# The last ten units of an attention kernel with a gated MLP: how the softmax sums, the PV lag and the last four output tiles are scheduled

## The chip, the cores and the metric

The kernel runs on one core of one Trainium2 chip. The metric is the device time in microseconds (us); the median of 3 runs is 1253.81 us (1253.02 to 1254.78).

## The reference

Everything is bf16 at the interface, with a sequence of 2048 tokens, a width of 512, 32 heads of 128 and 2048 cached keys.

```python
xn = layernorm(x)                                   # 2048 x 512
q = (xn @ wq) -> 32 heads x 2048 x 128
p = softmax(q @ k_cache.T * 128**-0.5)              # per head 2048 x 2048
s = concat_heads(p @ v_cache) @ wo                  # 2048 x 512
h = gelu(layernorm(xn) @ w1)                        # four column groups shifted by 1, -1, 2, -2 tokens
x1 = xn + shifted(h) @ w2
B = x1 + gelu(layernorm(x1) @ w3) @ w4              # width 1792 in between
out = x + s * silu(B)
```

## The kernel before

**Units and slots.** Attention is cut into 128 units of one head and 512 queries: `units` runs over 8 groups of four heads, in each over four query blocks (`qt`), in each over the four heads (`hh`). A unit has 8 slots (`SPU`), so the main loop has `NS` = 1024 of them. Below, 126.4 is slot 4 of unit 126. In each slot `s_slot` issues two score matmuls (128 keys by 512 queries each) into a two-bank PSUM tile from `psS` (two such tiles), and ScalarE turns them into `pT` with one exponential of 128x1024. `pv_slot` issues the two matmuls P times V of a slot that lies `LAG` or more slots back; `LAGS` lists the lag by position: 5 at the beginning, 10 in the long middle part, and back from 10 to 5 over units 120 to 122. Beside them a slot may carry matmuls of the next Q projection (`q_mm`, slots 0 and 1), of the output projection of one 128-token tile (`wo_mm`, slots 4 and 5), and pieces of the MLP (`chunks`, which run out in unit 119).

**Order.** All instructions are pinned to program order on their engine; the order is written out by the loop over `n`. What is put with `at(n, ...)` is issued at the end of slot n.

**Softmax sums.** VectorE adds the four `pT` tiles of a unit (`add_first`, `add_next` 2 and 3) and folds the result to 128x512 (`fold`). The sum over the 128 key partitions is then taken in one of two ways:

- *Turned units* (`turned(u)`: 4 <= u < `T1`, `T1` = 118): the folded tile is transposed by a DMA (`acc_turn`), VectorE reduces it to 128x4 (`turned_sums`) and takes the reciprocal, `dr` goes to DRAM, and `bcast` brings it back to all partitions (`rb`, 256 KB). `norm` of such a unit comes at slot 7 of unit u+2.
- *Other units* (0 to 3 and 118 to 127): `sums` issues four matmuls of one column each with `ones_t` and takes the reciprocal; `dr` and `rb` go by DMA in the same way, and `norm` comes at slot 2 of unit u+2.

The last unit has no folded tile: `split_sums` issues 40 one-column matmuls on the unfolded tiles between the last PV matmuls, and `bcast` follows.

**Output.** When the fourth head of a query block is normalised (`normed`), its four token tiles join `wo_todo`; `wo_mm` accumulates four heads in one PSUM bank and `wo_post` adds the bank to `s_acc`. For group 6, query blocks 2 and 3 are `deferred`: their `oT` goes to DRAM (`o_d`), comes back in `tail_open` as `oS`, and is accumulated into the same bank as group 7, which makes eight matmuls for tiles 8 to 15. In group 7 a tile is finished by `wo_out` (gate, residual, DMA out; `fin_load` brings its gate and residual). For tiles 12 to 15 `gate_sum` prepares `s_acc`, and the code behind the loop ends them with `last_scale` and `last_out`: tiles 12, 13 and 14 with 512 columns (the last add of 12 and 13 on GpSimd), tile 15 in two halves of 256. `tail_open` issues ten loads on SP at 121.0.

Of the kernel before, what the change touches and what calls it, by code (L numbers as in the profile page):

```python
# [17 lines left out]
def kernel(  # L18
# [102 lines left out]
    def mm(out, lhsT, rhs, start, stop):  # L121
        mm_count[0] += out.shape[-1] / 512
        pin(nc.tensor.matmul(out=out, lhsT=lhsT, rhs=rhs, start=start, stop=stop))  # L123
# [13 lines left out]
    LAGS = [(T0 * SPU + 4 * (i + 1), LAG + i) for i in range(5)] + [((T1 + 2) * SPU + 2, LAG + 5)]  # L137
    LAGS += [((T1 + 2) * SPU + 6 + 4 * i, LAG + 4 - i) for i in range(4)] + [(NS, LAG)]
# [95 lines left out]

    def sums(u):
        s = st[u]
        ps = psX.tile([P, 4], FP32, tag="xm" if u + 1 == QUIET - 1 else "xa", name="ps_sum")
        a = s["acc"][:, 0, :].rearrange("k (p j) -> k j p", j=4)
        for j in range(4):
            mm(ps[:, j:j + 1], a[:, j, :], ones_t[:], True, True)  # L240
        recip(s, ps)

    def recip(s, ps):
        rc = smp.tile([P, 4], FP32, name="rc")
        pin(nc.vector.reciprocal(out=rc[:], in_=ps[:]))
        s["dr"] = drp.tile([P, 4], FP32, name="dr")
        pin(nc.sync.dma_start(out=s["dr"][:], in_=rc[:]))

    def turned(u):
        return T0 <= u < T1  # L250
# [10 lines left out]
            out=sm[:], in_=s.pop("at")[:], axis=mybir.AxisListType.X, op=ALU.add))  # L261
        recip(s, sm)

    def split_sums(u, parts):
        s = st[u]
        if "ps" not in s:
            s["ps"] = psX.tile([P, 4], FP32, tag="xm", name="ps_sum")
        for a, first, last in parts:
            a = a.rearrange("k (p j) -> k j p", j=4)
            for j in range(4):  # L270
                mm(s["ps"][:, j:j + 1], a[:, j, :], ones_t[:], first and j == 0, last and j == 3)
        if parts[-1][2]:
            recip(s, s["ps"])

    def bcast(u):
        st[u]["rb"] = rp.tile([P, 512], FP32, name="rb")
# [20 lines left out]
    wo_box = {}  # L297

    def wo_mm(g, t, hhs, tag="xa"):
        if hhs[0] == 0:  # L300
            wo_box[0] = psX.tile([P, D], FP32, tag=tag, name="ps_wo")
        held = g == NG - 1 and (NG - 2, t // 4) in deferred
        if held and hhs[0] == 0:
            wo_part(wo_box[0][:], g - 1, t, range(HG), True, False)
        wo_part(wo_box[0][:], g, t, hhs, hhs[0] == 0 and not held, hhs[-1] == HG - 1)
# [10 lines left out]
    def tail_open():  # L316
        ph.close()
        ph3 = ph.enter_context(pool("ph3", reuse_waits="tile"))
        for g, qt in deferred:
            oTs[(g, qt)] = ph3.tile([P, HG, 512], BF16, name=f"oS{qt}")  # L320
            pin(nc.sync.dma_start(out=oTs[(g, qt)][:], in_=o_d[qt][:]))
        for t in range(4 * LQ, NT):
            gf = ph3.tile([P, D], BF16, name=f"gf{t}")
            pin(nc.sync.dma_start(out=gf[:], in_=g_d[t][:]))
            xf = ph3.tile([P, D], BF16, name=f"xf{t}")
            pin(nc.sync.dma_start(out=xf[:], in_=xsrc[t]))
            tl[t] = (gf, xf)

    def gate_sum(t):
        gf, xf = tl[t]  # L330
        sa = s_acc[:, t, :]
        pin(nc.vector.scalar_tensor_tensor(
            out=sa, in0=sa, scalar=0.5, in1=gf[:], op0=ALU.mult, op1=ALU.mult))
        pin(nc.vector.tensor_tensor(out=sa, in0=sa, in1=xf[:], op=ALU.add))

    def last_scale(t, ps, cs=slice(0, D)):
        gf, xf = tl[t]
        pin(nc.vector.scalar_tensor_tensor(  # L338
            out=gf[:, cs], in0=ps, scalar=0.5, in1=gf[:, cs], op0=ALU.mult, op1=ALU.mult))
# [15 lines left out]
    def wo_post(g, t):  # L355
        ps = wo_box.pop(0)
        sa = s_acc[:, t, :]
        if g == 0:
            pin(nc.vector.tensor_copy(out=sa, in_=ps[:]))
            return  # L360
        pin(nc.vector.tensor_tensor(out=sa, in0=ps[:], in1=sa, op=ALU.add))  # L361
# [409 lines left out]
            at((b - 4 - hh // 2) * SPU + (5, 7)[hh % 2], lambda h=h: load_wo(h))  # L771

    at(QUIET * SPU, tail_open)
    for t in range(4 * LQ, NT):
        if t % 4 < 2:
            at((QUIET + 1 + 2 * (t % 4)) * SPU + 4, lambda t=t: gate_sum(t))

    wo_todo = deque()
    pv_done = 0
# [11 lines left out]
    for n in range(NS):  # L791
# [33 lines left out]
            acc_turn(u - 1)  # L825
        if p == 2 and u >= 2 and turned(u - 2):
            bcast(u - 2)
        if p == (4 if u == T1 + 2 else 2) and u >= 2 and not turned(u - 2):
            normed(u - 2)
        if p == 3 and u >= 1 and not turned(u - 1):  # L830
            sums(u - 1)
        if p == 4 and u >= 1 and u != T1 + 1 and not turned(u - 1):
            bcast(u - 1)
        if p in (4, 5) and wo_todo:
            wo_mm(*wo_todo[0], (0, 1) if p == 4 else (2, 3))
# [9 lines left out]
        if u == QUIET - 1 and p >= 6:  # L845
            wo_mm(*wo_todo[0], (0, 1) if p == 6 else (2, 3), "xm")
            if p == 7:
                gg, t = wo_todo.popleft()
                wo_post(gg, t)
                at(n + 5, lambda t=t: wo_out(t))  # L850
        if p == 4:
            add_first(u)
        if p == 4 and u == NU - 1:
            a = st[u]["acc"]
            pin(nc.vector.tensor_tensor(out=a[:, 0:2, :], in0=a[:, 0:2, :], in1=a[:, 2:4, :], op=ALU.add))
        if p == 6 and u < QUIET:
# [26 lines left out]
            debt[0] += SMALL  # L883
        if p == SPU - 1 and u >= 2 and turned(u - 2):
            normed(u - 2)
        if p == SPU - 1 and u == T1 + 1:
            bcast(T1)
    while act_late:
        act_late.popleft()(NS)
    late = [fn for n in sorted(todo) for fn in todo[n]]  # L890
    assert min(todo) >= NS and not chunks and len(wo_todo) == 1
    U = NU - 1
    GL = NG - 1
    s = st[U]
    gg, t11 = wo_todo.popleft()
    ts = [4 * LQ + j for j in range(4)]
    norm(U - 1)
    held = range(HG)
    ready = range(HG - 1)
    pv_slot(U, 3)  # L900
    split_sums(U, [(s["acc"][:, i, :], i == 0, False) for i in range(2)]
               + [(s["pT"][2][:, i, :], False, False) for i in range(4)])
    pv_slot(U, 4)
    split_sums(U, [(s["pT"][3][:, i, :], False, False) for i in range(2)])
    pv_slot(U, 5)
    split_sums(U, [(s["pT"][3][:, i, :], False, i == 3) for i in range(2, 4)])
    bcast(U)
    for fn in late:
        fn()
    for t in ts[2:]:  # L910
        gate_sum(t)
    pv_slot(U, 6)
    pv_slot(U, 7)
    wo_mm(gg, t11, (0, 1, 2, 3))
    wo_post(gg, t11)
    wo_out(t11)
    pa = psS.tile([P, 2, 512], FP32, name="ps_s")
    pb = psS.tile([P, 2, 512], FP32, name="ps_s")
    pc = psX.tile([P, D], FP32, tag="xa", name="ps_wo")
    dst = [pa[:, 0, :], pb[:, 0, :], pc[:]]  # L920
    halves = [psX.tile([P, D], FP32, tag="xm", name="ps_wo"), psO.tile([P, D], FP32, tag="ps_o", name="ps_wo")]
    for j in (0, 1):
        wo_part(dst[j], GL - 1, ts[j], held, True, False)
        wo_part(dst[j], GL, ts[j], ready, False, False)
    wo_part(dst[2], GL - 1, ts[2], held, True, False)
    norm(U, 2)
    for j in (0, 1):
        wo_part(dst[j], GL, ts[j], (HG - 1,), False, True)
        last_scale(ts[j], dst[j])
        last_out(ts[j], nc.gpsimd)  # L930
    wo_part(dst[2], GL, ts[2], range(HG), False, True)
    last_scale(ts[2], dst[2])
    last_out(ts[2], nc.vector)
    for i, queue in enumerate((nc.sync, nc.scalar)):
        cs = slice(i * D // 2, (i + 1) * D // 2)
        ps = halves[i][:, cs]
        wo_part(ps, GL - 1, ts[3], held, True, False, cs)
        wo_part(ps, GL, ts[3], range(HG), False, True, cs)
        last_scale(ts[3], ps, cs)
        last_out(ts[3], nc.vector, cs, queue)  # L940
    ph.close()


# [28 lines left out]
```

## Time and profile before

| | us |
|---|---|
| median of 3 runs | 1253.81 |
| the profiled execution: its time | 1253.69 |
| the profiled execution: its span | 1251.9 |
| PE busy | 1242.8 (99%) |
| DVE busy (VectorE) | 1107.5 (88%) |
| ACT busy (ScalarE) | 1130.6 (90%) |
| POOL busy (GpSimd) | 139.5 (11%) |

The span goes from the first to the last instruction; 1.8 us of the time lie around it. L123 is the line of the matmul helper, so matmuls are told apart by their tiles. Busy times of one engine overlap a little: an instruction starts before the one in front of it has drained, so what a queue takes is read from start to start in the timeline (a 128x512 addition on VectorE lasts 0.69 us and the next one starts 0.60 us after it).

### The profile page before, as it was taken

Reading aid. Unit: us, or ns where it says so; the run is one execution under the profiler, and the core shown is the slowest. Engines: PE = TensorE matmul, PEld = TensorE weight load, DVE = VectorE, ACT = ScalarE, POOL = GpSimd, SP = SyncE. Lnnn points to the kernel's source line nnn. Section 1 sums busy time; section 2 is a strip of 40 time slices with the busy share of each in tenths; the row PEclk is TensorE's granted clock in tenths of the full one; section 3 lists DMA queues with packets and bytes.
Section 4 is the critical chain, followed back from the end, with each engine's and each line's share of the span. In section 5 each row is a group of like instructions: output and inputs, shape, how many; then the busy total and the mean of one; then the engine's idle time right before and its main releaser. Section 6 shows DMA issues by size and latency. Waiting matters only on the chain.

```text
span 1251.9 us, 16586 instructions
## 1 busy us (share of the span) xinstructions
PE 1242.8 (99%) x5872; PEld 599.1 (48%) x5872; DVE 1107.5 (88%) x1509; ACT 1130.6 (90%) x1285; POOL 139.5 (11%) x239
## 2 busy tenths in 40 slices
PE   9999999999999999999999999999999999999998
PEld 5444444444444444444444444444444444444444
DVE  7899999999899988899988889999888999888887
ACT  7999998888999888899988889998888999988893
POOL 4410003332101000000100000010000000000111
PEclk9999999999999999999999999999999999999999
DMA  9654444565635555344663345554535343564532
GB/s 185 136 114 88 78 106 80 118 149 109 135 72 114 118 95 102 61 91 90 111 126 76 69 93 97 110 71 108 97 89 108 66 89 81 115 134 74 154 72 69
DMA packets 235108, 126.70 MB, mean 101 GB/s; under 512 B 186832, under 2 KB 212048, under 8 KB 235024
## 3 DMA queue, kind: packets, MB, share of 16 engines
q1 hardware_dynamic: 225920, 100.40, 41.8%
q0 software_dynamic: 8672, 24.91, 7.9%
q8 instruction: 46, 0.75, 0.3%
q14 instruction: 38, 0.31, 0.1%
q10 hardware_dynamic: 432, 0.33, 0.1%
HBM read 82.58 MB, written 7.60 MB: 72 GB/s over the span
## 4 chain that ended last, share of the span: by engine, by line
PE 96%; DMA 1%; ACT 1%; DVE 1%; issue 0%; SPq 0%; POOL 0%; POOLq 0%; DVEq 0%
PE ps_s L123 35%; PE ps_o L123 34%; PE ps_m L123 10%; PE ps_q L123 9%; PE ps_wo L123 8%; ACT pT L207 1%; DMA dr<-rc 1%; DMA w_sb<-in_B_w_dram 0%; DMA rb<-dr 0%; PE ps_sum L123 0%; DVE gf L338 0%; DVE xf L343 0%; ACT pre L528 0%; DVE qT L193 0%; DVE bn L384 0%
## 5 line engine op out<-in xcount | busy, mean ns | idle before, releaser
L207 ACT ACTIVATE pT<-ps_s 128x1024 bf16<-128x1024 f32 x1024 | 1024.4, 1028 | 99.2 <-PE ps_s L123 88.7
L123 PE MATMUL ps_s<-qT,kT 128*128 128x512 bf16 x2048 | 608.9, 379 | 0.9 <-ACT pT L207 0.5
L123 PE MATMUL ps_o<-pT,vb 128*128 128x512 bf16 x2048 | 608.0, 379 | 0.3 <-DVE oT L294 0.3
L123 PEld LDWEIGHTS <-kT 128*128 128x128 bf16 x2048 | 231.1, 113 | 226.1 <-issue 4.9
L218 DVE TENSOR_TENSOR acc<-acc,pT 128x2048 bf16<-128x2048 bf16 x254 | 306.4, 1206 | 10.1 <-ACT pT L207 9.9
L123 PEld LDWEIGHTS <-vb 128*128 128x128 bf16 x2048 | 200.0, 98 | 225.8 <-DMA vb<-in_A_v_cache_dram 0.5
L213 DVE TENSOR_TENSOR acc<-pT 128x2048 bf16<-128x2048 bf16 x128 | 156.2, 1220 | 31.8 <-ACT pT L207 31.6
L123 PE MATMUL ps_q<-xnT,wq_h 128*128 128x512 bf16 (+1 forms) x524 | 152.8, 374 | 0.8 <-ACT xnT L459 0.6
L123 PE MATMUL ps_wo<-wo_h,oT 128*128 128x512 bf16 (+1 forms) x476 | 140.2, 377 | 0.2 <-DVE qT L193 0.2
L287 DVE TENSOR_TENSOR oT<-ps_o,rb 128x512 bf16<-128x512 f32 x114 | 122.3, 1073 | 8.9 <-DMA rb<-dr 8.9
L361 DVE TENSOR_TENSOR s_acc<-ps_wo,s_acc 128x512 f32<-128x512 f32 x100 | 68.7, 687 | 43.5 <-PE ps_wo L123 43.2
L222 DVE TENSOR_TENSOR acc<-acc 128x1024 bf16<-128x1024 bf16 x127 | 86.8, 683 | 0.9
L193 DVE CAST qT<-ps_q 128x512 bf16<-128x512 f32 x109 | 74.9, 688 | 8.7 <-PE ps_q L123 7.7
L123 PEld LDWEIGHTS <-wq_h 128*128 128x128 bf16 x524 | 50.8, 98 | 61.1 <-issue 1.3
L260 DVE TENSOR_REDUCE sm<-accT 128x4 f32<-128x512 bf16 x114 | 77.5, 680 | 0.5 <-DMA accT<-acc 0.2
L123 PE MATMUL ps_m<-xn2T,w_sb 128*128 128x512 bf16 x224 | 77.1, 379 | 0.0
L123 PE MATMUL ps_m<-w_sb,h2T 128*128 128x512 bf16 x224 | 77.1, 379 | 0.0
L123 PEld LDWEIGHTS <-oT 128*128 128x128 bf16 x484 | 47.3, 98 | 57.6 <-DVE oT L294 1.4
L659 POOL DMA_DIRECT2D w_sb<-in_B_w_dram x28 | 21.1, 754 | 370.4 <-PE ps_m L123 370.4
L687 POOL DMA_DIRECT2D g_d<-xr x16 | 8.7, 546 | 442.3 <-DVE xr L685 376.5
L223 DVE TENSOR_TENSOR acc<-acc 128x512 bf16<-128x512 bf16 x127 | 54.0, 425 | 4.4
L496 DVE SCALAR_TENSOR_TENSOR sq<-sq,pre 128x1024 bf16<-128x1024 bf16 x36 | 44.0, 1221 | 3.9 <-ACT sq L492 3.9
(89 smaller groups left out, 602.9 us busy)
## 6 DMA issues: line engine op xcount, KB each, us to landing
rb<-dr SPq DMA_DIRECT2D x128, 256.0 KB, 4.2
vb<-in_A_v_cache_dram SPq DMA_DIRECT2D x64, 256.0 KB, 3.6
w_sb<-in_B_w_dram POOLq DMA_DIRECT2D x28, 256.0 KB, 3.8
wo_h<-in_A_wo_dram SPq DMA_DIRECT2D x32, 128.0 KB, 3.0
wq_h<-in_A_wq_dram SPq DMA_DIRECT2D x28, 128.0 KB, 3.1
kT<-in_A_k_cache_dram SPq DMA_TRANSPOSE x128, 3.4
dr<-rc SPq DMA_DIRECT2D x128, 2.0 KB, 1.6
xr<-in_A_x_dram POOLq DMA_DIRECT2D x16, 128.0 KB, 2.5
```

The source lines that it names most:

```text
L123: pin(nc.tensor.matmul(out=out, lhsT=lhsT, rhs=rhs, start=start, stop=stop))
L193: pin(nc.vector.tensor_copy(out=qT[:], in_=st[u].pop("psq")[:]))
L207: pin(nc.scalar.activation(out=s["pT"][-1][:, jj:jj + 2, :], in_=sps[:], func=ACT.Exp, scale=SCALE))
L213: pin(nc.vector.tensor_tensor(out=s["acc"][:], in0=s["pT"][0][:], in1=s["pT"][1][:], op=ALU.add))
L218: pin(nc.vector.tensor_tensor(out=a[:], in0=a[:], in1=st[u]["pT"][i][:], op=ALU.add))
L222: pin(nc.vector.tensor_tensor(out=a[:, 0:2, :], in0=a[:, 0:2, :], in1=a[:, 2:4, :], op=ALU.add))
L223: pin(nc.vector.tensor_tensor(out=a[:, 0, :], in0=a[:, 0, :], in1=a[:, 1, :], op=ALU.add))
L260: pin(nc.vector.tensor_reduce(out=sm[:], in_=s.pop("at")[:], axis=mybir.AxisListType.X, op=ALU.add))
L287: pin(nc.vector.tensor_tensor(out=oTs[(g, qt)][:, hh, :].rearrange(f, j=4), in0=s["o"].rearrange(f, j=4), in1=s["rb"].rearrange("x (p j) - ...
L361: pin(nc.vector.tensor_tensor(out=sa, in0=ps[:], in1=sa, op=ALU.add))
L496: pin(nc.vector.scalar_tensor_tensor(out=sq[:].rearrange(f2), in0=sq[:].rearrange(f2), scalar=1.0, in1=pre[:].rearrange(f2), op0=ALU.add, ...
L659: pin(nc.gpsimd.dma_start(out=w[:], in_=w3_v[:, :, fc * P:(fc + 2) * P]))
```

## The change

- `T1` becomes 126: units 118 to 125 are turned units too. Only 126 still uses `sums`, at slot 4 of unit 127, with `bcast` at slot 5.
- The lag stays at 10 to the end of the loop, so ten PV slots (126.6, 126.7 and all of 127) come after it, where there were five.
- Unit 127 is summed by six matmuls of 512 columns with a 128x128 tile of ones (`ones_p`): the result stands in all partitions at once. VectorE takes the reciprocal of 128x512 from PSUM into `rb`; no DMA is in this path.
- Tiles 12 to 15 are all done in halves of 256 columns, each half in a PSUM bank of its own, each with `last_scale` and `last_out` on VectorE and its DMA out on SP or ACT in turn. GpSimd does no addition there. All of it stands behind the last PV matmul; before, most matmuls of tiles 12 to 14 stood ahead of the last `norm`.
- Unit 120 no longer carries two output tiles; tiles 0 to 3 go to units 118 to 121, 4 to 7 to 122 to 125, 8 and 9 to 126 and 127, 10 and 11 behind the loop. In 126 and 127 the held half of a tile goes to slots 2 and 3.
- The tail's loads are issued one pair at a time, at slot 5 of units 121 to 126; `gate_sum` of tiles 14 and 15 moves from behind the loop to 126.4 and 127.2. The last unit's third addition is made (`add_next(u, 2)` at 127.6).

```diff
-    T0, T1 = 4, NU - 10
...
+    T0, T1 = 4, NU - 2
+    LAGS = [(T0 * SPU + 4 * (i + 1), LAG + i) for i in range(5)] + [(NS, LAG + 5)]
...
-    def split_sums(u, parts):
+    def split_sums(u, parts, first, last):
         s = st[u]
...
+        if first:
+            s["ps"] = psS.tile([P, 2, 512], FP32, name="ps_s")[:, 0, :]
+        for i, a in enumerate(parts):
+            mm(s["ps"], tl["ones"][:], a, first and i == 0, last and i == len(parts) - 1)
+        if last:
+            s["rb"] = tl["rb"].tile([P, 512], FP32, tag="rb3", bufs=2, name="rb")
+            pin(nc.vector.reciprocal(out=s["rb"][:], in_=s["ps"]))
...
+    loads = [lambda t=t: gate_load(t) for t in range(4 * LQ, NT)]
+    for i, (g, qt) in enumerate(deferred):
+        loads.insert(2 + 3 * i, lambda g=g, qt=qt: held_load(g, qt))
+    for i, load in enumerate(loads):
+        at((QUIET + i) * SPU + 5, load)
     for t in range(4 * LQ, NT):
...
+        at((QUIET + 1 + 2 * (t % 4)) * SPU + 4 if t < NT - 1 else NS - 6, lambda t=t: gate_sum(t))
...
+        if p == (4 if u > T1 else 3) and u >= 1 and not turned(u - 1):
             sums(u - 1)
...
+        if p in (2, 3) and u >= NU - 2:
+            wo_held(*wo_todo[0], (0, 1) if p == 2 else (2, 3))
...
+        if p == 6 and u == NU - 1:
+            add_next(u, 2)
             a = st[u]["acc"]
             pin(nc.vector.tensor_tensor(out=a[:, 0:2, :], in0=a[:, 0:2, :], in1=a[:, 2:4, :], op=ALU.add))
...
+    acc = [s["acc"][:, i, :] for i in range(2)]
+    pT3 = [s["pT"][3][:, j, :] for j in range(4)]
+    split_sums(U, pT3[:2], True, False)
+    pv_slot(U - 1, 6)
+    split_sums(U, pT3[2:], False, False)
+    pv_slot(U - 1, 7)
+    late_sums = lambda: split_sums(U, acc, False, True)
     for fn in late:
         fn()
...
+    for tag in ("xa", "xm"):
+        gg, t = wo_todo.popleft()
+        wo_mm(gg, t, range(HG), tag)
+        if wo_todo:
+            late_sums()
+        wo_post(gg, t)
+        wo_out(t)
+        if wo_todo:
+            fin_load(t + 1)
+            norm(U - 1)
+    for p in range(SPU):
+        pv_slot(U, p)
     norm(U, 2)
...
+    parts = [(t, c, c + D // 2, q) for t in ts for c, q in ((0, nc.sync), (D // 2, nc.scalar))]
+    for (t, c0, c1, queue), ps in zip(parts, banks):
+        cs = slice(c0, c1)
+        wo_part(ps[:, cs], GL - 1, t, range(HG), True, False, cs)
+        wo_part(ps[:, cs], GL, t, range(HG), False, True, cs)
+        last_scale(t, ps[:, cs], cs)
+        last_out(t, nc.vector, cs, queue)
```

More of the change, by code (lines that the diff above doesn't have):

```diff
@@ L236, in sums @@
         s = st[u]
-        ps = psX.tile([P, 4], FP32, tag="xm" if u + 1 == QUIET - 1 else "xa", name="ps_sum")
+        ps = psX.tile([P, 4], FP32, tag="xa", name="ps_sum")
         a = s["acc"][:, 0, :].rearrange("k (p j) -> k j p", j=4)
@@ L262, in turned_sums @@
         recip(s, sm)
-    def split_sums(u, parts):
+    def split_sums(u, parts, first, last):
         s = st[u]
[L266 to L273, printed above, removed]
+        if first:
[5 more added lines that the diff above has]
+            pin(nc.vector.reciprocal(out=s["rb"][:], in_=s["ps"]))
     def bcast(u):
-        st[u]["rb"] = rp.tile([P, 512], FP32, name="rb")
+        st[u]["rb"] = (tl["rb"].tile([P, 512], FP32, tag="rb3", bufs=2, name="rb") if u >= T1 else rp.tile([P, 512], FP32, name="rb"))
         pin(nc.sync.dma_start(
@@ L299, in wo_mm, with wo_held @@
     def wo_mm(g, t, hhs, tag="xa"):
+        held = g == NG - 1 and (NG - 2, t // 4) in deferred
+        if held and 0 not in wo_box:
+            wo_held(g, t, range(HG), tag)
+        if hhs[0] == 0 and not held:
+            wo_box[0] = psX.tile([P, D], FP32, tag=tag, name="ps_wo")
+        wo_part(wo_box[0][:], g, t, hhs, hhs[0] == 0 and not held, hhs[-1] == HG - 1)
+    def wo_held(g, t, hhs, tag="xm"):
         if hhs[0] == 0:
             wo_box[0] = psX.tile([P, D], FP32, tag=tag, name="ps_wo")
[L302 to L305, printed above, removed]
+        wo_part(wo_box[0][:], g - 1, t, hhs, hhs[0] == 0, False)
     def wo_part(ps, g, t, hhs, first, last, cs=slice(0, D)):
@@ L318, in tail_open, with held_load, gate_load @@
         ph3 = ph.enter_context(pool("ph3", reuse_waits="tile"))
+        tl["rb"] = ph3
+        tl["ones"] = ph3.tile([P, P], BF16, name="ones_p")
+        pin(nc.gpsimd.memset(tl["ones"][:], 1.0))
         for g, qt in deferred:
             oTs[(g, qt)] = ph3.tile([P, HG, 512], BF16, name=f"oS{qt}")
-            pin(nc.sync.dma_start(out=oTs[(g, qt)][:], in_=o_d[qt][:]))
         for t in range(4 * LQ, NT):
[L323 to L327, printed above, removed]
+            tl[t] = [ph3.tile([P, D], BF16, name=f"{name}{t}") for name in ("gf", "xf")]
+    def held_load(g, qt):
+        pin(nc.sync.dma_start(out=oTs[(g, qt)][:], in_=o_d[qt][:]))
+    def gate_load(t):
+        for tile_, src in zip(tl[t], (g_d[t][:], xsrc[t])):
+            pin(nc.sync.dma_start(out=tile_[:], in_=src))
     def gate_sum(t):
@@ L890 @@
     late = [fn for n in sorted(todo) for fn in todo[n]]
-    assert min(todo) >= NS and not chunks and len(wo_todo) == 1
+    assert min(todo) >= NS and not chunks and len(wo_todo) == 2
     U = NU - 1
@@ L894 @@
     s = st[U]
-    gg, t11 = wo_todo.popleft()
     ts = [4 * LQ + j for j in range(4)]
[L897 to L906, printed above, removed]
@@ L918 @@
[L918 to L925, printed above, removed]
-    norm(U, 2)
[L927 to L930, printed above, removed]
@@ new lines @@
+    for p in range(SPU):
+        pv_slot(U, p)
+    norm(U, 2)
+    sb = [psS.tile([P, 2, 512], FP32, name="ps_s") for _ in range(2)]
+    banks = [b[:, 0, :] for b in sb]
+    banks += [psX.tile([P, D], FP32, tag=tag, name="ps_wo")[:] for tag in ("xa", "xm")]
+    banks += [psO.tile([P, D], FP32, tag="ps_o", name="ps_wo")[:] for _ in range(2)]
+    banks += [b[:, 1, :] for b in sb]
+    parts = [(t, c, c + D // 2, q) for t in ts for c, q in ((0, nc.sync), (D // 2, nc.scalar))]
[5 more added lines that the diff above has]
+        last_out(t, nc.vector, cs, queue)
```

39 lines of the change are left out of this document (3 added, 36 removed).

## The prediction

> **What bounds the kernel now.** I read the page first, then the chain of waits of the last 27 us, then the timeline of the last ten units, engine by engine.
>
> ```profile
> PE 1242.8 (99%) x5872; PEld 599.1 (48%) x5872; DVE 1107.5 (88%) x1509; ACT 1130.6 (90%) x1285; POOL 139.5 (11%) x239
> ...
> 1236.77 0.19 DVE rc L245
> 1236.98 2.64 DMA dr<-rc
> 1239.69 3.43 DMA rb<-dr
> 1243.14 0.44 DVE oT L294
> 1243.63 0.40 PE ps_s L123
> 1244.05 1.90 DVE gf L338 x3
> 1245.97 1.68 DVE xf L343
> 1247.65 0.35 DVE gf L338
> 1248.02 0.42 DVE xf L343
> ```
>
> TensorE is the bound almost everywhere: a 512-column matmul starts every 0.2157 us, and from 1139.8 to 1236 all gaps together are about 0.6 us. So only three things can move the time: matmul work, the gaps, and what stands behind the last matmul. The chain shows the one large gap: the last unit's sums go out and back by DMA (6.2 us), `norm` starts at 1243.14, and PE, which ran out of other work at 1243.06, goes on at 1243.63 (0.57 us lost). The end is VectorE's alone:
>
> ```profile
> 1244.83 2.27 POOL L343 TENSOR_TENSOR xf<-gf,s_acc 128x512 bf16<-128x512 bf16 x2 [19.08 <-DVE gf L338]
> 1245.97 1.68 DVE L343 TENSOR_TENSOR xf<-gf,s_acc 128x512 bf16<-128x512 bf16 x1
> 1246.24 0.60 PE L123 MATMUL ps_wo<-wo_h,oT 128*128 128x256 bf16 x4
> 1249.27 0.35 ACTq L344 DMA_DIRECT2D out_dram<-xf  x1
> ```
>
> The last four half matmuls (0.110 us each) end at 1246.68, the last DMA is issued at 1249.27: 2.59 us. VectorE's addition of 128x512 took 1.68 us while GpSimd did the same kind of addition; the same shape in L368 took 0.425.
>
> **The change, part by part; gains.**
> 1. Sums of 118 to 125 leave PE. From the timeline of unit 127:
>
> ```profile
> 1228.67 0.27 PE L123 MATMUL ps_sum<-ones_t,acc 128*128 128x1 bf16 x4
> 1228.80 0.60 PE L123 MATMUL ps_s<-qT,kT 128*128 128x512 bf16 x2
> ```
>
> They take 0.13 us of PE; eight units give -1.05.
> 2. Unit 127: the 40 one-column matmuls take 0.79, 0.27 and 0.25 us from start to start (1.31), six of 512 take 6 x 0.2157 = 1.29: 0.
> 3. Tiles 12 to 14 in halves: 16 x 0.110 instead of 8 x 0.2157 each, +0.03 x 3 = +0.1.
> 4. The DMA round trip goes, and with it 0.57, if nothing is late in its place (below).
> 5. Slots of four matmuls (0.863 us) run at ScalarE's pace (6.52 us for seven exponentials, 0.93), losing 0.05 each; units 126 and 127 have eight of them now and half as many later, as the held matmuls go to slots 2 and 3, against some shifted ones: -0.1.
> 6. End: from the last matmul 0.20 until VectorE starts (as at 1243.85 to 1244.05), then 0.44 + 0.42 for a half and 0.03 to the issue, 1.1 instead of 2.59: -1.5. PE makes a half in 8 x 0.110 = 0.88 us, VectorE in 0.79 (1247.58 to 1248.37), so PE sets the pace there.
>
> Gains: -3.1. At nothing I cost: the moved PV slots and tiles 3, 10 and 11 (as many matmuls as before); the spread loads (0.4 us on SP each, landing 5 us later, used a slot short of a unit later at the earliest; if late, VectorE's `gate_sum` waits); the ones' memset (POOL, some 60 us early); `fin_load` of tile 11 (behind the output of tile 8, needed some 9 us later); PSUM banks (the second half's bank waits for the reciprocal, which ends before it).
>
> **What VectorE must take over.** A turned unit adds a reduction (0.71 from start to start) and a slower `norm` (0.99 instead of 0.60). From start to start one unit is: additions 1.14 + 1.14 + 1.23, folds 0.72 + 0.35, `norm` 0.99, reduction 0.71, reciprocal 0.09, `wo_post` 0.60, `wo_out` 0.69 + 0.35 = 8.0 us; PE's unit of 40 matmuls is 8.63 + 0.05. `gate_sum` adds 1.33 in 122, 124, 126 and now 127. So VectorE's lateness behind PE goes: at 120.0 it is 1.8 (its `norm` of 117 ends at 1161.17, the unit began at 1159.38); unit 120 has 9.2 left (8.0, two MLP steps less one already done, a Q copy): 2.3; then 1.65, 2.3, 1.65, 2.3, 1.65, and 2.3 at 127.0. Unit 127 has 10.2 (with `gate_sum`, the third addition 1.14 and the half fold) against 9.0: 3.5 when the loop ends. Who waits: PV of 126.0, at 127.2, needs the bank that `norm` of 124 frees; PE gets there 2 x 0.92 + 0.43 = 2.3 after 127.0: a stall of 0.1. `sums` of 126 behind the folds: 0.1. Together +0.2.
>
> **Behind the loop.** PE has 42 matmuls to the last PV: 9.06 us, and reaches the first matmul that needs the last `norm` 7 x 0.110 later, at 9.83. VectorE: 3.5 late, `wo_out` of tile 9 to 4.5 (the sums are there at 18 x 0.2157 + 0.2 = 4.1), then the 128x512 RECIPROCAL R, then `wo_post` and `wo_out` of tile 10 (0.72 + 1.04), `norm` of 126 (0.60), the same for tile 11 (1.76): 4.1, then half a `norm`, 0.44. It is done at 9.0 + R, and PE waits R - 0.8.
>
> R is in no row. Nearest:
>
> ```profile
> L294 DVE TENSOR_TENSOR oT<-ps_o,rb 128x512 bf16<-128x512 f32 x13 | 8.9, 686 | 6.8 <-DMA rb<-dr 6.8
> L294 DVE TENSOR_TENSOR oT<-ps_o,rb 128x256 bf16<-128x256 f32 x2 | 0.8, 420 | 0.7 <-DMA rb<-dr 0.7
> L245 DVE RECIPROCAL rc<-ps_sum 128x4 f32<-128x4 f32 x14 | 2.5, 179 | 4.7 <-PE ps_sum L123 4.7
> L407 DVE TENSOR_SCALAR mvA<-nm 128x1 f32<-128x1 f32 x1 | 0.1, 146 | 0.0
> ```
>
> If a reciprocal streams like the product above, R = 0.69: PE waits for nothing. But 686 and 420 give 1.04 ns an element and 154 ns fixed, so the four elements of a RECIPROCAL cost 25 ns, 6 each: R = 154 + 512 x 6 = 3.2 us. With the one-element operation as the fixed part, 145 ns, they cost 8.4 each: 4.4 us. Two rows point to the slow kind, so I take R = 3.7, with 0.69 and 4.4 as ends. PE then waits 2.9. The sum is -3.1 + 0.2 + 2.9 = 0.0 on the profiled execution's 1253.69, 0.1 under the median of the runs: 1253.7. With R = 3.2 it is 1253.2, with 4.4 1254.4.
>
> [...]
>
> **The rivals.**
> - *A: a reciprocal streams at one element a cycle.* For it: every other 512-wide operation of VectorE takes 0.67 to 0.69 (1.07 with strides); against it: the 25 ns above. R = 0.69, no wait: -3.1 + 0.2 = -2.9, 1250.8.
> - *B, slower: the broadcast comes later than VectorE's queue.* In a turned unit the queue reaches `norm` 6.3 us after the reciprocal starts (0.09 + 1.23 + 1.07 + 1.04 + 1.14 + 1.14 + 0.60); `dr` and `rb` take 0.2 + 1.4 + 4.0 = 5.6 at the median landing of the middle part, 7.5 at its longest (5.9). Units 121, 123 and 125 have no `gate_sum` to cover it. VectorE has no idle time left to the end, so each wait arrives there: 3 x 1.2 = +3.6, 1257.3. It decides from a landing over 4.7 us on. For it: `norm` waited for `rb` in units 120 and 121 (0.3 and 1.4), beside the ten loads; against it: two waits (1.1 us) in 17 turned units before that, and fewer other transfers at the end.
> - *C: the stall halves the clock.* The granted clock after the last matmul (1246.8):
>
> ```profile
> 1248.00:1249.00 1.00, 0.00 (x0) 0.00 (x0) 0.94 (x3) 0.00 (x0) 0.00 (x0) 1.00 0.74 254
> 1249.00:1250.00 1.00, 0.00 (x0) 0.00 (x0) 0.24 (x1) 0.00 (x0) 0.00 (x0) 0.70 0.23 67
> 1250.00:1251.00 1.00, 0.00 (x0) 0.00 (x0) 0.00 (x0) 0.00 (x0) 0.00 (x0) 0.50 0.23 66
> ```
>
>   It fell to a half about 1249.4, after 2.6 us without a matmul; my stall is 2.9. If it falls then, a half costs PE 1.76 instead of 0.88; two halves so before it recovers are +1.8, 1255.5, with all eight +7. Against it: 0.57 us did nothing, and the fall need not meet the stall. [...]
>
> **How the numbers follow.** Forecast 0.46, A 0.24, B 0.15, C 0.15. About 0.2% (2.5 us) is what a measurement of this kernel can tell from no change: 1251.3 and 1256.3 are the bounds. Faster: most of A and a little of the forecast's low side, 0.22. Slower: most of B, a third of C, a little of the forecast, 0.19. Same: 0.59. The forecast's own range is 1252.4 to 1255.2 (R from 3.2 to 4.4, and 0.8 either way on VectorE's lateness); the whole range must reach A's middle and most of C and B: 1250.5 to 1256.8.
>
> **What would show it.** Right: one RECIPROCAL of 128x512 of 3 us or more; VectorE without idle time from about 120 on; PE idle 2 to 4 us ahead of the last unit's first half tile, released by L294; 1.1 us from the last matmul to the last issue; eight ps_sum groups gone. Wrong: a RECIPROCAL under 1 us; waits of L287 on `rb` over 0.5 us in the last units; a granted clock under 1.0 before the last matmul.

## The result and the profile after

| | before | after |
|---|---|---|
| median of 22 runs, us | 1253.57 (1252.52 to 1258.97) | 1254.85 (1253.39 to 1257.43) |
| the profiled execution: time, span | 1253.69, 1251.9 | 1253.95, 1252.2 |

The ratio is 1.0012 with a 95% interval of 1.0006 to 1.0017: the change makes the kernel slower, by 0.8 to 2.1 us. The two profiled executions differ by less than that, because the one after was 0.88 us ahead long before the part that the change touches (the addition to `s_acc` near 590 us, in code that the change doesn't touch, starts at 591.33 before and at 590.45 after; in ten of the traces of this case it starts between 590.19 and 592.41). Aligned there, the execution after ends 1.2 us later: its last VectorE instruction ends at 1249.57 against 1249.24, and 0.88 comes on top. The accounting below is against this 1.2.

The page of the kernel before, the chain that ended last (shares of the span):

```profile
PE 96%; DMA 1%; ACT 1%; DVE 1%; issue 0%; SPq 0%; POOL 0%; POOLq 0%; DVEq 0%
```

The page of the changed kernel, busy times and the same chain:

```profile
PE 1235.5 (99%) x5716; PEld 598.4 (48%) x5830; DVE 1120.5 (89%) x1526; ACT 1129.6 (90%) x1285; POOL 137.3 (11%) x238
...
PE 88%; DVE 6%; DMA 2%; ACT 2%; issue 1%; DVEq 0%; SPq 0%
```

Before, the chain was 96% TensorE and 1% VectorE; now it follows VectorE for 6% of the span (75 us). VectorE's busy total rose by only 13 us; it is its place on the path that changed. (Some matmul records are missing in this trace, 5716 for 5830 weight loads, so PE's busy time is not compared.)

The waits of the changed kernel from 1140 to 1253 us (engine and line, what it waited for: us in total, times, longest):

```profile
PE ps_s L123 <- DVE oT L292: 1.8, 1, 1.8
PE ps_o L123 <- DVE oT L285: 1.3, 3, 0.5
DVE oT L285 <- DMA rb<-dr: 0.9, 2, 0.5
```

Three places. The first is the tail. The timeline of VectorE behind the loop (start, duration, engine, line, what):

```profile
1232.37 1.06 DVE L285 TENSOR_TENSOR oT<-ps_o,rb 128x512 bf16<-128x512 f32 x1
1233.35 0.68 DVE L374 SCALAR_TENSOR_TENSOR gl<-s_acc,gl 128x512 bf16<-128x512 f32 x1
1234.06 0.43 DVE L376 TENSOR_TENSOR xl<-gl,xl 128x512 bf16<-128x512 bf16 x1
1234.41 3.35 DVE L271 RECIPROCAL rb<-ps_s 128x512 f32<-128x512 f32 x1
1237.67 0.63 DVE L369 TENSOR_TENSOR s_acc<-ps_wo,s_acc 128x512 f32<-128x512 f32 x1
...
1241.79 0.75 DVE L292 TENSOR_TENSOR oT<-ps_o,rb 128x256 bf16<-128x256 f32 x2
```

TensorE leaves the loop at 1230.10. VectorE, which is late from the loop, starts the wide reciprocal 4.3 us behind that, and it takes 3.35 us. Two output tiles and the `norm` of 126 stand in its queue behind it, and only then the first half of the last `norm`, at 1241.79. TensorE ran out of other work before that:

```profile
1239.65 0.78 PE L123 MATMUL ps_s<-wo_h,oT 128*128 128x256 bf16 x3
1242.26 0.28 PE L123 MATMUL ps_s<-wo_h,oT 128*128 128x256 bf16 x1 [1.83 <-DVE oT L292]
```

Without the wait the next matmul would have started at 1239.98, so the gap is 2.28 us (the profile's 1.83 counts from the modelled end of the matmul in front). Of it 0.27 stands ahead of the third matmul of the first row, which needs the `norm` of 126, and 2.01 ahead of the fourth.

The second place is the turned units 125 to 127; the timeline there, both engines:

```profile
1204.46 1.07 DVE L285 TENSOR_TENSOR oT<-ps_o,rb 128x512 bf16<-128x512 f32 x1 [0.33 <-DMA rb<-dr]
...
1205.59 0.59 PE L123 MATMUL ps_o<-pT,vb 128*128 128x512 bf16 x2 [0.54 <-DVE oT L285]
...
1214.00 0.59 PE L123 MATMUL ps_o<-pT,vb 128*128 128x512 bf16 x2 [0.34 <-DVE oT L285]
...
1223.35 0.59 PE L123 MATMUL ps_o<-pT,vb 128*128 128x512 bf16 x2 [0.41 <-DVE oT L285]
```

The first `norm` ends at 1205.53, and the PV matmul that needs the bank it frees starts at 1205.59. With the starts read against TensorE's pace this costs 0.50, 0.50 and 0.57 us in the slots 125.2, 126.2 and 127.2, 1.57 together. The first line also shows the third place: this `norm` itself had waited 0.33 us for its broadcast. So had one before it, while TensorE was in unit 122:

```profile
1177.12 1.07 DVE L285 TENSOR_TENSOR oT<-ps_o,rb 128x512 bf16<-128x512 f32 x1 [0.53 <-DMA rb<-dr]
```

The end is as the prediction had it: the last four half matmuls end at 1248.50, and VectorE's last addition

```profile
1249.15 0.42 DVE L351 TENSOR_TENSOR xf<-gf,s_acc 128x256 bf16<-128x256 bf16 x1
```

ends 1.07 us later, where it was 2.56 before (2.59 to the start of the last DMA issue).

### The profile page after: what moved, and what is told of

It reads as the page before. It is cut to its first block, busy times and chain, and to the rows that moved or that the text cites. A ratio compares the mean times of both kernels' runs of the same rounds, so it can differ in the third digit from the quotient of the medians.

```text
span 1252.2 us, 16413 instructions
## 1 busy us (share of the span) xinstructions
PE 1235.5 (99%) x5716; PEld 598.4 (48%) x5830; DVE 1120.5 (89%) x1526; ACT 1129.6 (90%) x1285; POOL 137.3 (11%) x238
## 4 chain that ended last, share of the span: by engine, by line
PE 88%; DVE 6%; DMA 2%; ACT 2%; issue 1%; DVEq 0%; SPq 0%
PE ps_o L123 32%; PE ps_s L123 31%; PE ps_m L123 10%; PE ps_q L123 8%; PE ps_wo L123 7%; ACT pT L206 2%; DMA rb<-dr 1%; DVE acc L217 1%; DVE oT L285 1%; DMA dr<-rc 1%; DVE acc L212 1%; DVE gl L374 0%; DVE sm L259 0%; DVE s_acc L369 0%; DVE acc L221 0%
## 5 line engine op out<-in xcount | busy, mean ns | idle before, releaser
L123 PE MATMUL ps_o<-pT,vb 128*128 128x512 bf16 x2014 | 600.7, 379 | 5.0 <-DVE oT L285 1.3
L123 PE MATMUL ps_s<-qT,kT 128*128 128x512 bf16 x1992 | 596.8, 379 | 2.3 <-ACT pT L206 0.5
L285 DVE TENSOR_TENSOR oT<-ps_o,rb 128x512 bf16<-128x512 f32 x122 | 130.7, 1071 | 7.9 <-DMA rb<-dr 7.8
L259 DVE TENSOR_REDUCE sm<-accT 128x4 f32<-128x512 bf16 x122 | 82.8, 678 | 0.1
```

The lines of the kernel that those rows point to most:

```text
L259: pin(nc.vector.tensor_reduce(out=sm[:], in_=s.pop("at")[:], axis=mybir.AxisListType.X, op=ALU.add))
L285: pin(nc.vector.tensor_tensor(out=oTs[(g, qt)][:, hh, :].rearrange(f, j=4), in0=s["o"].rearrange(f, j=4), in1=s["rb"].rearrange("x (p j) - ...
```

## The experiments

Two theories were tested from the start. **V**: the gain is real and is spent on VectorE's queue, on the wide reciprocal in the tail and on the work of the turned units in front of the norms. **B**: the norms are late because their broadcasts land late. **C** is the prediction's rival C, the clock after the stall. **P** is about the end alone: that the additions on GpSimd explain its length. Diffs are against the changed kernel unless said; times are medians of 11 runs, and ratios are to runs of the kernel before on the same chip.

The medians carry the spread of what runs before (590.19 to 592.41 near 590 us), and many of their intervals overlap. So the table adds, from the one trace of each kernel, the stretch from the start of `add_first` in unit 117 (ahead of everything that the versions do differently) to the end of VectorE's last instruction. It is 112.93 us in the kernel before and 114.15 in the changed one.

| kernel | ratio to before | stretch, us against the changed kernel |
|---|---|---|
| before | 1 | -1.22 |
| e1_copy | 0.9991 | -2.27 |
| e9_nogate | 0.9999 | -1.74 |
| e2_t120 | 1.0019 | -0.20 |
| e4_t120_early | 1.0006 | -1.08 |
| e3_early | 1.0012 | +1.36 (the clock fell, see there) |
| e5_dma | 1.0007 | -1.05 |
| e6_slot5_dma | 0.9989 | -3.43 |
| e7_slot5_recip | 0.9993 | -2.56 |
| e10_slot4_dma | 0.9984 | -3.58 |
| e11_dma_first | 0.9990 | -3.03 |
| e8_before_nopool | 1.0004 | -1.15 (+0.07 against the kernel before) |

### The reciprocal taken out: e1_copy

```diff
-            pin(nc.vector.reciprocal(out=s["rb"][:], in_=s["ps"]))
+            pin(nc.vector.tensor_copy(out=s["rb"][:], in_=s["ps"]))
```

> The 128x512 RECIPROCAL of the last unit is replaced by a copy of the same shape from the same PSUM bank; the last unit's softmax is so left without its reciprocal, and its output is not the reference's. Theory V (VectorE's queue spends the gain: a 3.35 us reciprocal behind the loop, and PV waits before it): the copy takes about 0.7 us, VectorE reaches the last norm about 2.6 us sooner, PE's gap of 2.3 us ahead of the last unit's first half goes to under 0.2, and the kernel is 2.1 to 2.3 us faster than the changed one, some 0.9 us under the kernel before (ratio 0.9993). The PV waits in units 125 to 127 (1.5 us in all) stay. Rival O (the loss is the new order: nothing of the last tiles stands ahead of the last norm, so whatever is late there shows): the gap shrinks little, since VectorE would be late by its other work (wo_post, wo_out, norm of 126) as well; under 0.5 us is won, ratio 1.0008 or more.

1253.0 us, ratio 0.9991 (0.9982 to 0.9999). Its timeline:

```profile
1235.16 0.68 DVE L271 COPY rb<-ps_s 128x512 f32<-128x512 f32 x1
```

The same shape, same source and same destination take 0.68 us as a copy and 3.35 as a reciprocal, so the price is the operation's, not that of PSUM or fp32. There is no gap ahead of the half tiles, while the PV waits stay (0.14 to 0.76 in single units, about 1.5 together): the two losses are separate. Against the changed kernel it gains 1.85 us by the medians and 2.6 by the two ratios (0.0021 of 1253.6); the gap of 2.28 lies between, and so does the stretch of the trace. Rival O allowed under 0.5.

### VectorE's work lightened: e9_nogate

```diff
-    for t in range(4 * LQ, NT):
-        at((QUIET + 1 + 2 * (t % 4)) * SPU + 4 if t < NT - 1 else NS - 6, lambda t=t: gate_sum(t))
```

> The changed kernel without gate_sum of tiles 12 to 15; the gate and residual of these tiles are so left out of s_acc and the output of 512 tokens is not the reference's. VectorE has 1.33 us less in units 122, 124, 126 and 127. Theory V (VectorE's work makes it late): the PV waits of units 125 to 127 (1.5 us) fall under 0.4, and the reciprocal behind the loop starts 0.2 us sooner: 1.3 to 1.6 us faster than the changed kernel, ratio to before about 1.0000. Rival B (the broadcasts land late and set the turned units' norm): norm still ends where rb lands, the PV waits keep 1 us or more, ratio 1.0008 or more.

1253.64 us, ratio 0.9999 (0.999 to 1.0008): 1.2 us below the changed kernel, and 1.6 by the ratios against the runs of their own chips. The waits of this kernel:

```profile
PE ps_s L123 <- DVE oT L292: 1.8, 1, 1.8
```

The PV waits are gone, and the gap in the tail stays (2.12 us by the starts). The turned units, their DMAs and their broadcasts are all there; only 4 x 1.33 us of VectorE's work is missing. So the PV waits need VectorE's full queue, as V has it; B alone, with the broadcasts as the limit, would have kept them. (One `norm` still waits 0.54 us for its broadcast here, and nothing on TensorE waits for that `norm`.)

### Six units turned back: e2_t120 and e4_t120_early

```diff
-    T0, T1 = 4, NU - 2
+    T0, T1 = 4, NU - 8
...
-        if p == 2 and u >= 2 and not turned(u - 2):
+        if p == (SPU - 1 if u >= T1 + 2 else 2) and u >= 2 and not turned(u - 2):
...
```

The sums of 120 to 125 stay on TensorE, at slot 3 as in the kernel before. e4 moves `late_sums` ahead of the own half of tile 10 as well.

> T1 = 120 in the changed kernel: units 120 to 125 go back to one-column matmuls for their sums (at slot 3 of the next unit), with norm still at slot 7 of unit u+2 and all else as changed. Theory V: VectorE has 1.1 us less in each of six units, is late by less than 1 us at the heads of units 125 to 127, and the PV waits on its norm (0.50, 0.50, 0.57 us) go; the sums cost 0.13 x 6 = 0.8 us of PE, of which about half returns because the exponentials' gaps of 0.09 us shrink; the reciprocal is held by the matmuls with ones and starts at most 0.3 us sooner. Together -1.0 to -1.4 us against the changed kernel, ratio to before about 1.0002. Rival S (taking the sums off PE is a clear gain and the PV waits come from late broadcasts): 0.5 to 0.8 us slower than the changed kernel, ratio 1.0017.

e2: 1256.84 us, ratio 1.0019 (1.001 to 1.0028). V's ratio of 1.0002 is missed, and the figure is that of rival S, 1.0017, whose mechanism is not what the trace shows. The PV waits went, as V said, but a wait took their place that V had not seen:

```profile
PE ps_s L123 <- DVE oT L292: 1.8, 1, 1.8
PE ps_sum L123 <- DVE acc L222: 1.0, 1, 1.0
```

At 121.3 the one-column matmuls of unit 120 stand in TensorE's queue ahead of the slot's scores, and VectorE's second fold ends only at 1174.29: VectorE is late here already, at the end of the MLP, and TensorE waits 1.15 us by the starts. Turned units hide exactly this, since nothing on TensorE waits for their folds (in the changed kernel TensorE waits for none of theirs). And the tail did not get shorter with a VectorE that was less late, because the reciprocal then waited 1.50 us for the last ones-matmuls, which stand behind all of tile 10:

```profile
1236.03 3.36 DVE L271 RECIPROCAL rb<-ps_s 128x512 f32<-128x512 f32 x1 [1.50 <-PE ps_s L123]
```

By its trace e2 is no worse than the change (0.20 us shorter in the table), while its median is 2.0 us higher. Four of its eleven runs have a mean granted clock of 0.998 and took 1256.95 to 1257.84 us; the median of the other seven is 1255.46. So part of the 2.0 goes with the clock (see e3), and the rest is not explained.

> As e2, and the last two matmuls with ones are moved between the held and the own half of tile 10, 0.9 us earlier, so that the reciprocal can start sooner. Theory V: with VectorE on time at the end of the loop the reciprocal starts about 1 us sooner, and the gap ahead of the last half tiles falls from 2.3 to about 1.2 us: 1.0 us under e2, 2.0 to 2.4 under the changed kernel, ratio to before 0.9993 to 0.9996. Rival O: no gain over e2, since the wo_out work between the reciprocal and the last norm only moves.

e4: 1254.38 us, ratio 1.0006 (0.9997 to 1.0014). With the ones-matmuls earlier the reciprocal starts 3.28 us behind the loop instead of 4.3, and the gap is 1.26, against V's 1.2. The wait at 121.3 stays, and by about as much V's ratio of 0.9993 to 0.9996 is missed. Rival O, no gain over e2, is out.

### Only the ones-matmuls earlier: e3_early

```diff
+    wo_held(*wo_todo[0], range(HG), "xa")
+    late_sums()
...
-        if wo_todo:
-            late_sums()
```

> The changed kernel with the last two matmuls with ones moved between the held and the own half of tile 10, 0.9 us earlier, and nothing else. Theory V: VectorE, not the sums, sets the start of the reciprocal (4.3 us behind the loop, right behind wo_out of tile 9), so it starts where it did and nothing moves: within 0.3 us of the changed kernel, ratio to before 1.001 to 1.0014. Rival M (the reciprocal waits for the matmuls with ones): 0.9 us faster, ratio 1.0005. Beside e2 and e4, where the same move came with VectorE on time.

1254.77 us, ratio 1.0012 (1.0003 to 1.0021), the same as the changed kernel. The reciprocal still starts at 1234.12, right behind `wo_out` of tile 9. So in the changed kernel it is VectorE's queue that ends last there, not the sums; in e2 it was the sums. Both have to be early, as in e4.

This profiled execution (1255.36 us, mean granted clock 0.998) also shows rival C. Its windows of 1 us (busy share of PE and number of matmuls first; the last three columns are granted clock, DMA share and GB/s):

```profile
1241.00:1242.00 1.00, 0.02 (x1) 0.03 (x2) 0.97 (x4) 0.00 (x0) 0.00 (x0) 1.00 0.00 0
1242.00:1243.00 1.00, 1.00 (x7) 0.82 (x8) 0.92 (x3) 0.00 (x0) 0.00 (x0) 0.70 0.38 131
1243.00:1244.00 1.00, 1.00 (x7) 0.69 (x6) 0.44 (x2) 0.00 (x0) 0.00 (x0) 0.50 0.00 0
1244.00:1245.00 1.00, 1.00 (x7) 0.69 (x6) 0.59 (x2) 0.00 (x0) 0.00 (x0) 0.50 0.22 66
1245.00:1246.00 1.00, 1.00 (x7) 0.75 (x6) 0.52 (x2) 0.00 (x0) 0.00 (x0) 0.59 0.22 66
1246.00:1247.00 1.00, 1.00 (x12) 0.90 (x10) 0.75 (x2) 0.00 (x0) 0.00 (x0) 1.00 0.00 0
```

TensorE has work again from 1241.98; 0.4 us into it the clock falls to a half and stays there until about 1245.8 (an estimate from the 0.70 and the 0.59 of the windows). Groups of four half-width matmuls start 0.85 us apart instead of 0.44, and the five groups in that stretch lose 0.11 + 0.41 + 0.41 + 0.41 + 0.30 = 1.6 us. In the profiled execution of the changed kernel a gap of the same length left the clock at 1.00. The other runs carry the clock only as a mean, which is 0.998 in this execution. In 4 of the 22 runs of the changed kernel it is 0.998 too, and these took 1255.99 to 1257.43 us; the median of the other 18 is 1254.64. The same mean stands in 4 of 11 runs of e2, 5 of e3 and 2 of e9, the other kernels whose gap in the tail is over 2 us (2.12 to 2.28), and in none of the 77 runs of e1, e4, e5, e6, e7, e10 and e11, where it is under 1.7.

### The change with its DMA back: e5_dma

```diff
-            mm(s["ps"], tl["ones"][:], a, first and i == 0, last and i == len(parts) - 1)
+            a = a.rearrange("k (p j) -> k j p", j=4)
+            for j in range(4):
+                mm(s["ps"][:, j:j + 1], a[:, j, :], ones_t[:], first and i == 0 and j == 0,
+                   last and i == len(parts) - 1 and j == 3)
...
-            pin(nc.vector.reciprocal(out=s["rb"][:], in_=s["ps"]))
+            recip(s, s["ps"][:, 0:4])
+            bcast(u)
```

> The changed kernel with the last unit summed by one-column matmuls, a 128x4 reciprocal and the round trip by DMA, at the same places in the order (the no-DMA part alone undone). Theory V: the round trip of some 6.2 us starts about 4.5 us behind the loop and lands 10.7 to 11.0 behind it, where PE needs the half norm at 9.8: a gap of 1.3 to 1.6 us instead of 2.3, so 0.7 to 1.0 us faster than the changed kernel (ratio to before 1.0003 to 1.0006): the round trip is cheaper than the wide reciprocal in a queue that is late. Rival D (the round trip was the wait that had to go): a gap of 2.5 us or more, slower than the changed kernel.

1254.42 us, ratio 1.0007 (0.9998 to 1.0016). Everything else of the change stays; only the last unit's sums go out and back by DMA again:

```profile
1241.78 0.76 DVE L295 TENSOR_TENSOR oT<-ps_o,rb 128x256 bf16<-128x256 f32 x2 [2.09 <-DMA rb<-dr]
1242.26 0.28 PE L123 MATMUL ps_s<-wo_h,oT 128*128 128x256 bf16 x1 [1.47 <-DVE oT L295]
```

VectorE now has time left and waits 2.09 us for the broadcast, and TensorE's gap is 1.62 by the starts, at the upper end of V's 1.3 to 1.6. By the traces the DMA trip, started as late as it is here, costs less than the reciprocal that replaced it (a gap of 1.62 against 2.28, a stretch 1.05 shorter); the intervals of the two ratios overlap. Rival D, a gap of 2.5 or more, is out.

### Both put right: e6_slot5_dma, e7_slot5_recip, e10_slot4_dma

e6 takes the sums of 120 to 125 by matmul at slot 5 (two slots later than in e2, so that the fold is done), in a PSUM bank that is free there; it has the DMA sums of e5, and `late_sums` stands ahead of tile 10. e7 is e6 with the ones-matmuls and the wide reciprocal of the change. e10 is e6 with the sums at slot 4.

```diff
-    T0, T1 = 4, NU - 2
+    T0, T1 = 4, NU - 8
...
-        ps = psX.tile([P, 4], FP32, tag="xa", name="ps_sum")
+        ps = psX.tile([P, 4], FP32, tag="xm" if T1 <= u < NU - 3 else "xa", name="ps_sum")
...
-        if p == (4 if u > T1 else 3) and u >= 1 and not turned(u - 1):
+        if p == (4 if u > NU - 2 else 5 if u > T1 else 3) and u >= 1 and not turned(u - 1):
...
+    late_sums()
...
-        if wo_todo:
-            late_sums()
```

> T1 = 120 in the changed kernel, with the one-column sums of units 120 to 125 at slot 5 of the next unit (in e2 they stood at slot 3 and PE waited 1.15 us at the first of them for a fold that VectorE had not reached), the last unit summed by one-column matmuls and the DMA round trip, and its last sums ahead of tile 10. Theory V: no PV wait (-1.6 us against the changed kernel), the sums of six units +0.8 less 0.4 of gaps that close, and the round trip lands some 9 us behind the loop, before the last PV, so the 2.3 us gap goes: 3.0 to 3.5 us faster than the changed kernel, ratio to before 0.998 to 0.9988. Rival O (the order behind the last norm costs by itself): 0.9995 or more.

e6: 1251.51 us, ratio 0.9989 (0.998 to 0.9998), the first whole version with an interval under 1, just above V's 0.998 to 0.9988. Against the changed kernel its stretch is 3.43 us shorter, where V had 3.0 to 3.5. No wait of TensorE for VectorE is left in the last 110 us, and there is no gap in the tail.

> As e6, but with the matmuls with ones and the 128x512 reciprocal as in the change. Theory V: VectorE starts the reciprocal 2.6 us behind the loop and reaches the last norm at about 10.4, so a gap of 0.5 us stays: 0.4 to 0.6 us slower than e6, ratio to before 0.9984 to 0.9992; 2.5 to 3 us faster than the changed kernel. Rival O: as e4, 1.0003 or more.

e7: 1252.49 us, ratio 0.9993 (0.9985 to 1.0002). The reciprocal starts 2.55 us behind the loop, as early as VectorE's own queue allows, and a gap of 0.53 us is left (V: 0.5; its ratio of 0.9984 to 0.9992 is just missed). So none of the orders tried here hides the wide reciprocal; this one misses it by half a microsecond. The times alone do not tell e7 from e6, their intervals overlap.

> As e6 with the one-column sums of units 120 to 125 at slot 4 instead of 5, ahead of the output projection's matmuls. In e6 PE still shows a gap of 0.09 us per unit ahead of the scores of slot 5, beside the 0.13 us of the sums at that slot. If PE's pace there is ScalarE's (a score matmul waits for the exponential two slots back), the sums fill that gap at slot 4, and 0.09 x 5 = 0.4 to 0.5 us is won over e6, ratio to before 0.9984 to 0.9987, unless VectorE's fold is late at 121.4 and costs up to 0.3. If the sums cost their full time wherever they stand: as e6, 0.9989.

e10: 1251.11 us, ratio 0.9984 (0.9975 to 0.9993), the lowest of all versions; its interval overlaps that of e6, and its stretch is 0.15 us shorter. Its timeline in the tail:

```profile
1233.29 0.17 DVE L244 RECIPROCAL rc<-ps_s 128x4 f32<-128x4 f32 x1
...
1239.60 0.75 DVE L295 TENSOR_TENSOR oT<-ps_o,rb 128x256 bf16<-128x256 f32 x2 [0.92 <-PE ps_o L123]
```

The narrow reciprocal is out at 1233.46; the broadcast is back in time, and VectorE waits for TensorE's last PV matmul, not the other way round. The DMA trip that the change removed is hidden completely once it starts early enough: the narrow reciprocal stands 2.69 us behind the loop here (1233.29 against 1230.60) and 4.30 in e5 (1235.37 against 1231.07). In e6 each of the units 121 to 125 has a gap of 0.09 us ahead of the slot with the sums, 0.45 together; at slot 4 these are gone, but for 0.29 in 121 where the fold is still late. They come from slots of four matmuls, where ScalarE's exponentials set the pace (0.93 us a slot against 0.863 for the matmuls); a sum there fills time that TensorE would wait anyway.

### All units turned, but the DMA trip first: e11_dma_first

```diff
+    wo_held(*wo_todo[0], range(HG), "xa")
+    late_sums()
...
-        if wo_todo:
-            late_sums()
```

with the DMA sums of e5. `T1` stays at 126. The 128x4 reciprocal then stands ahead of `wo_out` of tile 9.

> The changed kernel (T1 = 126 as in the change) with the last unit summed by one-column matmuls and the DMA round trip, these sums between the halves of tile 10 and the 128x4 reciprocal ahead of wo_out of tile 9 on VectorE. Theory V: the reciprocal starts 3.3 us behind the loop, when VectorE has done its norm of 125; the round trip lands 9.7 behind it; the gap ahead of the last half tiles falls from 2.3 to about 0.3; the PV waits of units 125 to 127 (some 1.5 us) stay. 2.0 us faster than the changed kernel, ratio to before 0.9994 to 0.9998; the 0.8 to 1.1 us between it and e6 are what the turned sums of units 120 to 125 cost on VectorE's queue. Rival O: 1.0005 or more.

1251.81 us, ratio 0.999 (0.9981 to 0.9999), better by its middle than V's 0.9994 to 0.9998, which its interval still holds. The waits of this kernel:

```profile
PE ps_o L123 <- DVE oT L288: 0.4, 1, 0.4
PE ps_s L123 <- DVE oT L295: 0.2, 1, 0.2
```

The narrow reciprocal starts 3.25 us behind the loop, by the starts the gap in the tail is 0.40, and the PV waits are 0.07 and 0.57 where the changed kernel's execution had 1.57 with the same work in the loop. So the PV waits differ from one execution to the next (0.64 here; 1.57, 1.47, 1.36 and 1.47 in the changed kernel, e1, e3 and e5, which have the same work in the loop). They go with the waits for broadcasts: in these units `norm` waited 0.34 us for `rb` in e11, and 0.9 to 1.1 in the other four. Its interval overlaps those of e6 and e10, so whether 8 turned units or 2 are better is not settled by these runs.

### GpSimd's part of the end before: e8_before_nopool

The only edit of the kernel before: the additions of tiles 12 and 13 go to VectorE.

```diff
-        last_out(ts[j], nc.gpsimd)
+        last_out(ts[j], nc.vector)
```

> The kernel before with one edit: the last additions of tiles 12 and 13 on VectorE instead of GpSimd. Theory P (the 1.68 us of VectorE's addition of 128x512 was a collision with GpSimd's): that addition falls to 0.42, two additions of 0.35 come onto VectorE, and the kernel ends 0.5 to 0.6 us sooner, ratio 0.9995. Rival Q (the addition is slow for another reason, such as its own data): 0.7 us later, 1.0006.

1254.01 us, ratio 1.0004 (0.9995 to 1.0013): no gain. Its timeline has

```profile
1248.10 0.69 DVE L343 TENSOR_TENSOR xf<-gf,s_acc 128x512 bf16<-128x512 bf16 x1
...
1250.41 0.35 ACTq L344 DMA_DIRECT2D out_dram<-xf  x1
```

The addition takes 0.69 without GpSimd beside it and took 1.68 with it, so the collision cost 1.0 us, not the 1.26 that I had from the 0.425 of another line of the same shape. VectorE's two added additions cost more than that: from the end of the last matmul (1247.34) to this issue it is 3.07 us, and it was 2.59. In this execution the wait ahead of the last `norm`'s matmuls was 0.38 us shorter (0.18 against 0.56), so the stretch as a whole is the same. P fell: taking GpSimd out of the end does not shorten it. What is left as the cause of the shorter end in the changed kernel is that VectorE gets its work in halves, each as soon as it is made; that was not tried by itself.

## Why the prediction was wrong

The forecast was no change (0.0); the runs say +1.3, with 0.8 as the lower end. The working took 2.5 us as the least that can be told from no change, and 22 runs of each kernel told 1.3. Point by point:

| step of the prediction | forecast, us | measured, us |
|---|---|---|
| 1. sums of 118 to 125 off PE | -1.05 | -1.05, but see 5 |
| 2, 3. tail sums; tiles in halves | 0, +0.1 | as forecast |
| 4. the wait ahead of the last `norm` | -0.57 | gone, replaced by the gap |
| 5. ScalarE-paced gaps | -0.1 | +0.3 |
| 6. the end | -1.5 | -1.5 (2.56 to 1.07) |
| `sums` of 126 behind the folds | +0.1 | +0.09 |
| PV waits for the late `norm` | +0.1 | +1.57 |
| gap ahead of the last unit's half tiles | +2.9 | +2.28 |
| sum | 0.0 | +1.2 |

The sum of the right column is 1.2, the aligned traces differ by 1.2, and the medians by 1.3. That the forecast was not further off is in part luck: the gap in the tail came out 0.6 smaller than forecast, against 1.9 that went the other way.

**The step that failed is VectorE's lateness and the PV wait that follows from it.** The working had 1.65 and 2.3 us at the heads of the units in turn, and a stall of 0.1 in one place. Measured at the heads of 121 to 127: 2.2, 2.3, 2.9, 2.4, 3.4, 2.6, 2.7. TensorE reaches the bank that PV needs 2.3 us into units 126 and 127, as the working has it, and 3.0 us into 121 to 125, where the first two slots carry a Q projection as well. So 3.4 in 125, 2.6 in 126 and 2.7 in 127 are each past it, and these are the three units that wait. The sum of VectorE's durations was not what was off; the term that the sum put at nothing is the waits inside VectorE's queue. Two norms waited for their broadcast, 0.53 us while TensorE was in 122 and 0.33 in 125, on a landing of 7.1 and 8.0 us after the reciprocal, where the working had 5.6. VectorE has no idle time to catch up (from 1172 us to its end the profile lists no other wait of it), so each wait stays to the end. e11 shows it most plainly: its one wait of 0.34 comes in 122, and from there to 127 it is 2.1 and 2.7 late in turn, where the working had 1.65 and 2.3, and 0.57 is lost at 127.2. This is rival B, at a quarter of its price; e9 shows that it needs the full queue to hurt. In a loop with two engines this near to each other I should have carried the spread of the durations, not their medians. That the PV waits would go with prompt broadcasts and the queue as it is was not tried.

**The ScalarE-paced gaps (5) had the wrong sign.** A slot of four matmuls takes TensorE 0.863 us (4 x 0.2157) and ScalarE 0.93 (6.52 for seven exponentials). Taking 0.13 us of sums out gives part of it back as waiting: 0.07 to 0.09 in each of the units 121 to 124, and 0.04 at three more unit heads, the end of the loop counted as one. e10 shows the counterpart, the sums put where that gap is.

**The gap in the tail was right in mechanism and mis-sized.** R came out at 3.35 us against 3.7, below the value taken and inside its bounds: (3350 - 154) / 512 = 6.2 ns an element, so the estimate from the four-element reciprocal (6 ns, 3.2 us) was the better of the two rows, and rival A is out. (What the working put in its favour, that every other 512-wide operation takes 0.67 to 0.69, was misread: additions of bf16 alone take 0.42.) VectorE's lateness at the start of the reciprocal was 4.3 against 4.5.

**Rival C is partly true.** It priced two halves at half clock at +1.8; e3's execution shows about +1.6. In the changed kernel the mean clock of 0.998 stands in 4 of 22 runs, and without these the median is 0.2 lower; in e3 and e2 it stands in 5 and 4 of 11 runs, and moves theirs more. In e3 it stood at a half for about 3.4 us (1242.4 to 1245.8), from 0.4 us after the end of a gap of 2.28 us on; what sets that length no run shows.

**What stays open.** Why the broadcasts of two units landed 1.5 to 2.4 us later than the working's 5.6: in one case `dr` alone took 3.2 us from its issue to that of `rb`, in the other the tail's loads were issued beside it; neither was tried by itself. And what sets whether the clock falls in a run with a gap of over 2 us.

## What to carry to other kernels

Before work is moved onto an engine that is 88% busy, sum its queue over each single unit and compare it with the slack to the first instruction that waits for it; where the slack is below the spread of the durations and of the DMA landings (here 7.1 and 8.0 us where the working had 5.6), count a wait. In this kernel the operation that left DMA for VectorE stood in that engine's queue until 4.3 us behind the loop and left a gap of 2.28 us, where the DMA trip at the same place left 1.62 (e5). The trip's latency went by starting it earlier: the narrow reciprocal and a DMA trip, started 1.6 us sooner, left TensorE no wait (e10), and the wide reciprocal cost at least 0.5 us in each of the orders tried. And of the work taken off TensorE part came back as waiting, 0.07 to 0.09 us in each of four units, in slots where ScalarE sets the pace (0.93 us against 0.863).

## What the hardware showed unexpectedly

- A reciprocal of 128x512 fp32 from PSUM took 3.35 us (the changed kernel), a copy of the same shape 0.68 (e1).
- Behind a gap of 2.28 us on TensorE the granted clock stood at 0.50 for about 3.4 us in one execution (e3) and at 1.00 in another (the changed kernel, which differs from e3 in the place of two matmuls); the fall came 0.4 us after work had resumed.
- Two additions whose profile lines name the same shapes, 128x512 bf16, took 0.69 (L343 in e8) and 0.425 us (L368 in the kernel before): the slower one reads `s_acc`, which other rows give as f32 and this row's shape does not show. That this is the cause was not tried.
